# Transposing a convolution's output by DMA through HBM in place of TensorE, in a fused convolution and feed-forward kernel

## The chip, the cores and the metric

The kernel runs on one core of one Trainium2 chip. The metric is device time in microseconds (us), the median of several runs of the whole launch. A profile of one execution shows the engines apart: PE is TensorE's matmul stream and PEld its weight loads, DVE is VectorE, ACT is ScalarE, POOL is GpSimd, and SP is the engine that issues most of the DMAs. "SPq" rows are the DMA issues on SP.

## The reference

The input x is 8 sequences of 3904 rows of 192 features, in fp32. A softmax over 7 taps for each of 8 heads gives the weights of a causal convolution along the sequence: 24 features belong to one head and share its taps. What comes out goes, row by row, through a gated feed-forward network without a nonlinearity.

```python
# convolution: w = softmax(weight) of shape (8 heads, 7 taps), 6 rows of zeros ahead of each sequence
out = np.einsum('hk,bskhg->bshg', w, x_unf)      # then reshaped to (31232, 192)
# network
a = x @ w1            # 192 -> 1024
b = x @ w2            # 192 -> 1024
h = a * b @ w3        # 1024 -> 1024
return (h @ w_out)    # 1024 -> 192, fp32
```

## The kernel before

All matmuls are in bf16. The two last products are folded: the kernel multiplies w3 by w_out once (lines 305 to 324), so each row of a * b needs a single product with a 1024 x 192 matrix W.

**Two tilings.** The convolution works in 32 blocks of 976 rows (BLK = 8 windows of 122 rows). The network works in 61 chunks of 512 rows (CH). Between them lies a ring of 4096 columns, in which the convolved rows stand transposed: features on partitions, rows along the free axis.

**The convolution of a block** (`band_products`, lines 229 to 235, and `conv_pair`, lines 186 to 201). A window is 128 input rows on 128 partitions, 122 of them new. For each head a banded 128 x 122 matrix holds the taps. Eight matmuls (line 193), two heads to a PSUM bank, make all eight windows; four ACT copies (line 197) bring them to SBUF as bf16 into the tile `convo`, 122 partitions by 8 windows by 256 columns. Then one POOL copy (line 201) repeats features 128 to 191 in columns 192 to 255. After that the next block's x is cast to bf16 on POOL (line 180) and the load of x for the block three further on is issued on SP (line 76).

**The transposes of a block** (`transposes`, lines 237 to 239, and `transp`, lines 209 to 226). For each of two groups of 128 columns, eight TensorE transposes (line 213) write one PSUM bank, and DVE copies it to the ring (line 218). The first group gives xT0 (features 0 to 127), the second xT2 (features 128 to 191, twice). A third operand, xT1, is xT0 with its halves of 64 partitions exchanged: from block 2 on, two DMAs on SP make it out of xT0 (lines 223 and 224); for blocks 0 and 1, an ACT and a DVE copy do (lines 220 and 221).

**Why three operands.** In `first_product` (lines 261 to 276) a matmul for a takes partitions 0 to 63 and one for b takes partitions 64 to 127, side by side in TensorE's rows. Each of the three operands gives both a slice of 64 features. Eight groups of six matmuls (line 270) make one chunk; ACT copies a (line 275), and DVE multiplies it with b (line 276). `second_product` (lines 280 to 297) multiplies with W in two halves of 16 matmuls (line 289), ACT copies (line 292), and SP stores the chunk (line 294).

**The order is written out by hand.** Every engine executes its instructions in the order of the program. The main loop (lines 363 to 373) runs over chunks c = 3 to 60: `first_product(c)`, then a convolution step if one is due, the first half of `second_product(c - 3)`, a further step if due, the second half. The steps stand in a list (lines 241 to 247): the products of block it + 1 come ahead of the transposes of block it. A step is due in chunk c when chunk c + 2 needs it: what chunk c transposes is read for the first time by `first_product(c + 2)`. So in most pairs of chunks the first has both steps, the products of block it + 1 and the transposes of block it, and the second has none. Of the 32 transposes, those of blocks 0, 1 and 2 stand ahead of the loop, and those of blocks 3 to 31 in it.

**Waits between DMAs.** The program has eight DMA semaphores, used in turn; a DMA that reuses one waits on SP until the DMA that had it before has landed.

Of the kernel before, what the change touches and what calls it, by code (L numbers as in the profile page):

```python
# [10 lines left out]
BF16 = mybir.dt.bfloat16  # L11
# [6 lines left out]
def kernel(  # L18
# [10 lines left out]
    nc = tc.nc  # L29

    B, S, D = x.shape
# [6 lines left out]
    ST = 122  # L38
    NW = 8
    BLK = ST * NW  # L40
# [4 lines left out]
    RING = 8 * CH  # L45
    LAG = 3

    const = ctx.enter_context(tc.tile_pool(name="const", bufs=1))
    stage = ctx.enter_context(tc.tile_pool(name="stage", bufs=2))
    work = ctx.enter_context(tc.tile_pool(name="work", bufs=2))  # L50
    psum = ctx.enter_context(tc.tile_pool(name="psum", bufs=8, space=bass.MemoryType.PSUM))
    ctx.enter_context(tc.manual_schedule())

    def bank(shape, dtype, name):
        return psum.tile(shape, dtype, tag="bank", name=name)
# [51 lines left out]
    for jt in range(JT):  # L107
# [11 lines left out]
        out=dmask, in_=ones.unsqueeze(2).to_broadcast([128, K, ST]),  # L119
# [9 lines left out]
    for q, (c0, j0, n) in enumerate(QC):  # L129
# [6 lines left out]
        out=wsb, in0=wsb, in1=wmax.unsqueeze(2).to_broadcast([128, H, K]),  # L136
# [6 lines left out]
        out=wsb, in0=wsb, in1=wsum.unsqueeze(2).to_broadcast([128, H, K]),  # L143
# [21 lines left out]
                nc.scalar.copy(out=dst, in_=src)  # L165


    xT0 = const.tile([128, RING], BF16)
    xT1 = const.tile([128, RING], BF16)
    xT2 = const.tile([128, RING], BF16)  # L170
    xT = (xT0, xT1, xT2)

    def cast_x(it, first=False):
        xb = work.tile([128, NW, D], BF16, tag="xb", bufs=2, name="xb")
# [6 lines left out]
        return xb  # L181

    convo_of = {}
    xb_of = {}

    def conv_pair(it, t):
        if t == 0:
            convo_of[it] = work.tile([128, NW, D + 64], BF16, tag="convo", bufs=2, name="convo")
        convo, xb = convo_of[it], xb_of[it]
        cps = bank([128, 2, NW, G], FP32, "cps")  # L190
        for r in range(2):
            h = 2 * t + r
            nc.tensor.matmul(  # L193
                cps[0:ST, r], Aband[:, h, :], xb[:, :, h * G:(h + 1) * G],
                start=True, stop=True)
        dst = convo[0:ST, :, 2 * t * G:(2 * t + 2) * G]
        nc.scalar.copy(  # L197
            out=dst.rearrange("s b (r g) -> s r b g", r=2), in_=cps[0:ST])
        if t == 3:
            del xb_of[it]  # L200
            nc.gpsimd.tensor_copy(out=convo[0:ST, :, D:D + 64], in_=convo[0:ST, :, 128:192])  # L201

    def ring_spans(t0, n):
        a = t0 % RING
        if a + n <= RING:
            return [(0, a, n)]
        return [(0, a, RING - a), (RING - a, 0, n - (RING - a))]

    def transp(it, k):
        convo = convo_of[it]  # L210
        tps = bank([128, BLK], BF16, "tps")
        for w in range(NW):
            nc.tensor.transpose(  # L213
                out=tps[:, w * ST:(w + 1) * ST],
                in_=convo[0:ST, w, 128 * k:128 * (k + 1)],
                identity=ident[0:ST, 0:ST])
        for src, a, n in ring_spans(it * BLK, BLK):
            nc.vector.tensor_copy(out=xT[2 * k][:, a:a + n], in_=tps[:, src:src + n])  # L218
            if k == 0 and it < 2:
                nc.scalar.copy(out=xT1[0:64, a:a + n], in_=tps[64:128, src:src + n])  # L220
                nc.vector.tensor_copy(out=xT1[64:128, a:a + n], in_=tps[0:64, src:src + n])  # L221
            elif k == 0:
                nc.sync.dma_start(out=xT1[0:64, a:a + n], in_=xT0[64:128, a:a + n])
                nc.sync.dma_start(out=xT1[64:128, a:a + n], in_=xT0[0:64, a:a + n])
        if k == 1:
            del convo_of[it]


    def band_products(it):
        for t in range(4):  # L230
            conv_pair(it, t)
        if it + 1 < NB:
            xb_of[it + 1] = cast_x(it + 1)
        if it + 3 < NB:
            xr_of[it + 3] = load_x(it + 3)

    def transposes(it):
        transp(it, 0)
        transp(it, 1)

    steps = [(band_products, 0), (transposes, 0), (band_products, 1)]
    ready = {0: 2}
    for it in range(1, NB):
        if it + 1 < NB:
            steps.append((band_products, it + 1))
        steps.append((transposes, it))
        ready[it] = len(steps)
# [159 lines left out]
```

## Time and profile before

| what | value |
|---|---|
| median of 3 runs | 586.35 us (586.03 to 587.52) |
| span of the profiled execution, first to last instruction | 584.6 us |
| granted TensorE clock, mean | 0.996 |
| PE transposes, line 213 | 512 matmuls, mean 222 ns of one |
| DVE copies of them, line 218, 128 x 976 | 50, mean 661 ns of one |
| POOL copy, line 201 | 32, mean 612 ns of one |
| DMA | 64.17 MB, mean 110 GB/s |

The profile gives one time for the execution on the device and another for the span from the first instruction to the last; the runs' median lies 1.75 us above the span. A row of the timeline starts with start and duration in us, then the engine, the line and operation, output and input, and how many instructions are merged in the row. In square brackets stands how long the engine was idle before it and who released it. The duration of one matmul includes its way through the array; neighbours overlap, so what matmuls take of the time is read from their starts, or from the chain of work that ended last, where each has its own share alone. A row of DMA issues ends with the size in KB (of 1024 bytes) and the median us from issue to landing. A row of windows gives the busy time of PE, PEld, DVE, ACT and POOL in a stretch, then the granted TensorE clock, the share of 16 DMA engines, and GB/s.

### The profile page before, as it was taken

The numbers are of one execution on the slowest core, as the hardware profiler recorded it, in microseconds if no ns is written. First come the engines' busy times: TensorE is split into PE (matmuls) and PEld (weight loads), VectorE is DVE, ScalarE is ACT, GpSimd is POOL, SyncE is SP. The second block draws the span as 40 slices with busy tenths as digits, with TensorE's granted clock in tenths as the row PEclk, the third lists the DMA queues.
The fourth block names the chain that finished last, engine by engine and source line by source line (L and its number), as shares of the span: only waits on it lengthen the run. The fifth ranks groups of instructions, "written<-read, shape, count | busy, mean of one in ns | idle before, by whom it ended". The sixth has DMA issues, their size and how long they took to land.

```text
span 584.6 us, 14554 instructions
## 1 busy us (share of the span) xinstructions
PE 557.5 (95%) x5776; PEld 358.3 (61%) x5776; DVE 374.9 (64%) x590; ACT 405.3 (69%) x761; POOL 78.8 (13%) x94
## 2 busy tenths in 40 slices
PE   0869999999999999999999999999999999999997
PEld 0346765666656756656656656666666666566657
DVE  6447576575676666675765666766766756766760
ACT  2567686677676776776776776776866777766672
POOL 3352101111101201111001111021011111010000
PEclk9989999999999999999999999999999999999999
DMA  7992033244343442344342343353332441221213
GB/s 192 349 287 73 15 113 106 69 123 127 89 120 98 128 126 74 98 126 116 91 126 72 100 126 99 111 143 93 115 106 67 126 126 35 66 73 46 72 56 109
DMA packets 74793, 64.17 MB, mean 110 GB/s; under 512 B 3690, under 2 KB 72932, under 8 KB 74724
## 3 DMA queue, kind: packets, MB, share of 16 engines
q1 hardware_dynamic: 74100, 62.42, 36.9%
q10 hardware_dynamic: 624, 0.82, 0.6%
q8 instruction: 45, 0.74, 0.6%
q14 instruction: 24, 0.20, 0.1%
HBM read 31.74 MB, written 23.99 MB: 95 GB/s over the span
## 4 chain that ended last, share of the span: by engine, by line
PE 91%; issue 3%; DVE 2%; POOL 1%; ACT 1%; DMA 1%; ACTq 0%; SPq 0%; POOLq 0%; DVEq 0%
PE pa L270 52%; PE ops L289 28%; PE tps L213 4%; PE cps L193 4%; PE pb L270 1%; PE wps L322 1%; DMA xr<-in_x_dram 1%; DVE abT L276 1%; POOL xb L180 0%; PE w3ps L313 0%; POOL wb L332 0%; DVE cprod L152 0%; ACT w3b L307 0%; DVE xT L218 0%; DVE w3T L316 0%
## 5 line engine op out<-in xcount | busy, mean ns | idle before, releaser
L276 DVE TENSOR_TENSOR abT<-asb,pb 128x512 bf16<-128x512 bf16 x488 | 318.1, 687 | 141.3 <-PE pb L270 136.8
L270 PE MATMUL pa<-xT,wb 64*128 64x512 bf16 x1464 | 330.2, 378 | 1.2 <-ACT xT L220 0.7
L270 PE MATMUL pb<-xT,wb 64*128 64x512 bf16 x1464 | 330.2, 378 | 0.6 <-DVE xT L221 0.3
L275 ACT CAST asb<-pa 128x512 bf16<-128x512 f32 x488 | 285.2, 586 | 48.0 <-PE pb L270 21.9
L270 PEld LDWEIGHTS <-wb 64*128 64x128 bf16 x2928 | 139.2, 94 | 173.6 <-issue 17.6
L289 PE MATMUL ops<-W_sb,abT 128*128 128x192 bf16 x1952 | 175.5, 246 | 0.0
L289 PEld LDWEIGHTS <-abT 128*128 128x128 bf16 x1952 | 159.7, 98 | 12.3 <-issue 12.3
L292 ACT COPY osb<-ops 128x384 f32<-128x384 f32 x122 | 58.3, 478 | 104.3 <-PE ops L289 104.1
L201 POOL COPY convo<-convo 122x512 bf16<-122x512 bf16 x32 | 19.6, 612 | 433.6 <-ACT convo L197 417.6
L218 DVE COPY xT<-tps 128x976 bf16<-128x976 bf16 (+7 forms) x78 | 40.7, 569 | 44.3 <-PE tps L213 44.3
L197 ACT CAST convo<-cps 122x384 bf16<-122x384 f32 x128 | 52.3, 504 | 2.7 <-PE cps L193 2.7
L193 PE MATMUL cps<-xb,Aband 128*122 128x192 bf16 x256 | 29.3, 259 | 18.8 <-POOL xb L178 15.3
L180 POOL CAST xb<-xr 128x1536 bf16<-128x1536 f32 x31 | 45.5, 1467 | 0.0
L193 PEld LDWEIGHTS <-Aband 128*122 128x122 bf16 x256 | 22.9, 138 | 31.7 <-issue 17.0
L213 PE MATMUL tps<-ident,convo 122*128 122x122 bf16 x512 | 34.4, 222 | 1.4 <-ACT convo L197 1.3
L213 PEld LDWEIGHTS <-convo 122*128 122x128 bf16 x512 | 31.0, 101 | 2.4 <-ACT convo L197 1.6
L322 PE MATMUL wps<-wo_b,w3T 128*128 128x192 bf16 x64 | 6.6, 246 | 1.2 <-DVE w3T L316 1.1
L316 DVE COPY w3T<-w3ps 128x1024 bf16<-128x1024 bf16 x8 | 5.4, 689 | 2.9 <-PE w3ps L313 2.9
L324 ACT CAST W_sb<-wps 128x192 bf16<-128x192 f32 x8 | 2.5, 319 | 6.2 <-PE wps L322 6.2
L322 PEld LDWEIGHTS <-w3T 128*128 128x128 bf16 x64 | 5.1, 98 | 1.6 <-DVE w3T L316 1.6
L138 ACT ACT_TABLE_LOAD x1 | 1.3, 1283 | 6.3 <-DMA xr<-in_x_dram 6.3
L165 ACT COPY Aband<-cband 32x152 bf16<-32x152 bf16 (+1 forms) x4 | 1.2, 306 | 6.0 <-DVE cband L158 5.9
(36 smaller groups left out, 44.3 us busy)
## 6 DMA issues: line engine op xcount, KB each, us to landing
xr<-in_x_dram SPq DMA_DIRECT2D x31, 768.0 KB, 5.4
out_dram<-osb SPq DMA_DIRECT2D x61, 384.0 KB, 3.0
xT<-xT SPq DMA_DIRECT2D x46, 122.0 KB, 2.3
w3f<-in_moe_w_dram SPq DMA_DIRECT2D x8, 512.0 KB, 9.8
wo_f<-in_moe_w_out_dram SPq DMA_DIRECT2D x1, 768.0 KB, 9.1
xr<-in_x_dram SPq DMA_DIRECT2D x1, 672.0 KB, 7.6
w0f<-in_moe_w_dram ACTq DMA_DIRECT2D x2, 128.0 KB, 6.0
w1f<-in_moe_w_dram ACTq DMA_DIRECT2D x2, 128.0 KB, 5.9
```

Of the source, the lines that this page charges most:

```text
L180: nc.gpsimd.tensor_copy(out=xb, in_=xr)
L193: nc.tensor.matmul(cps[0:ST, r], Aband[:, h, :], xb[:, :, h * G:(h + 1) * G], start=True, stop=True)
L197: nc.scalar.copy(out=dst.rearrange("s b (r g) -> s r b g", r=2), in_=cps[0:ST])
L201: nc.gpsimd.tensor_copy(out=convo[0:ST, :, D:D + 64], in_=convo[0:ST, :, 128:192])
L213: nc.tensor.transpose(out=tps[:, w * ST:(w + 1) * ST], in_=convo[0:ST, w, 128 * k:128 * (k + 1)], identity=ident[0:ST, 0:ST])
L218: nc.vector.tensor_copy(out=xT[2 * k][:, a:a + n], in_=tps[:, src:src + n])
L270: nc.tensor.matmul(dst, wb[k][rows, ft * 128:(ft + 1) * 128], xT[k][rows, r0:r0 + CH], start=(k == 0), stop=(k == 2))
L275: nc.scalar.copy(out=asb, in_=pa)
L276: nc.vector.tensor_tensor(out=ab[:, ft, :], in0=asb, in1=pb, op=ALU.mult)
L289: nc.tensor.matmul(ops[:, r, :], ab[:, jt, g * 128:(g + 1) * 128], W_sb[:, jt, :], start=(jt == 0), stop=(jt == JT - 1))
L292: nc.scalar.copy(out=osb[:, 2 * half:2 * half + 2, :], in_=ops)
L322: nc.tensor.matmul(wps, w3T[:, gt, :], wo_b[:, gt, :], start=(gt == 0), stop=(gt == JT - 1))
```

## The change

Blocks 0 and 1 stay as they are, with the exchange of halves on ACT and DVE. From block 2 on, POOL makes two more copies into `convo`, which becomes 384 columns wide: the columns 256 to 383 then hold features 0 to 127 with their halves exchanged. Two DMAs on SP (112 partitions and 10) write the block's 976 rows of 384 columns to a buffer in HBM, of which there are three. Where the transposes of the block stood, one transposing DMA on SP (two, where the block wraps round the ring's end) reads 976 x 384 from HBM and writes 128 partitions x 3 x 976 into the ring. The ring's three operands become one tile. The TensorE transposes, their DVE copies and the two exchanging DMAs are gone for these blocks.

The built program has SP's queue in this order for a pair of chunks: rows of block it + 1 (two DMAs), x of block it + 4, the transposing DMA of block it, the stores of two chunks. The rows wait for the last of the three POOL copies of block it + 1. The first matmul of `first_product(c + 2)` waits for the transposing DMA that was issued in chunk c.

```diff
+    dram = ctx.enter_context(tc.tile_pool(name="dram", bufs=3, space=bass.MemoryType.DRAM))
...
-    xT0 = const.tile([128, RING], BF16)
-    xT1 = const.tile([128, RING], BF16)
-    xT2 = const.tile([128, RING], BF16)
-    xT = (xT0, xT1, xT2)
+    xTa = const.tile([128, 3, RING], BF16)
+    xT = [xTa[:, k, :] for k in (0, 2, 1)]
+    xT1 = xT[1]
+
+    PE_BLOCKS = 2
+    C = 2 * D
...
-            convo_of[it] = work.tile([128, NW, D + 64], BF16, tag="convo", bufs=2, name="convo")
+            convo_of[it] = work.tile([128, NW, C], BF16, tag="convo", bufs=2, name="convo")
...
             nc.gpsimd.tensor_copy(out=convo[0:ST, :, D:D + 64], in_=convo[0:ST, :, 128:192])
+            if it >= PE_BLOCKS:
+                nc.gpsimd.tensor_copy(out=convo[0:ST, :, 256:320], in_=convo[0:ST, :, 64:128])
+                nc.gpsimd.tensor_copy(out=convo[0:ST, :, 320:384], in_=convo[0:ST, :, 0:64])
+                rows = dram.tile([NW, ST, C], BF16, tag="rows", bufs=3, name="rows")
+                rows_of[it] = rows
+                for a, b in ((0, 112), (112, ST)):
+                    nc.sync.dma_start(out=rows[:, a:b, :].rearrange("w s c -> s w c"),
+                                      in_=convo[a:b])
+                del convo_of[it]
...
-            if k == 0 and it < 2:
+            if k == 0:
                 nc.scalar.copy(out=xT1[0:64, a:a + n], in_=tps[64:128, src:src + n])
                 nc.vector.tensor_copy(out=xT1[64:128, a:a + n], in_=tps[0:64, src:src + n])
-            elif k == 0:
-                nc.sync.dma_start(out=xT1[0:64, a:a + n], in_=xT0[64:128, a:a + n])
-                nc.sync.dma_start(out=xT1[64:128, a:a + n], in_=xT0[0:64, a:a + n])
...
     def transposes(it):
+        if it >= PE_BLOCKS:
+            rows = rows_of.pop(it).rearrange("w s c -> (w s) c")
+            for src, a, n in ring_spans(it * BLK, BLK):
+                nc.sync.dma_start_transpose(out=xTa[:, :, a:a + n], in_=rows[src:src + n, :])
+            return
         transp(it, 0)
         transp(it, 1)
```

More of the change, by code (lines that the diff above doesn't have):

```diff
@@ L183 @@
     convo_of = {}
+    rows_of = {}
     xb_of = {}
```

## The prediction

> **What bounds the kernel now.** I read the shares of the engines first, then the chain of work that ended last.
>
> ```profile
> PE 557.5 (95%) x5776; PEld 358.3 (61%) x5776; DVE 374.9 (64%) x590; ACT 405.3 (69%) x761; POOL 78.8 (13%) x94
> ...
> PE 91%; issue 3%; DVE 2%; POOL 1%; ACT 1%; DMA 1%; ACTq 0%; SPq 0%; POOLq 0%; DVEq 0%
> ```
>
> PE sets the end nearly alone; ACT and DVE have about a third of the span to spare. So a matmul that goes is worth its full length, provided that its data still come in time. Next comes PE's timeline for one pair of chunks in mid-run:
>
> ```profile
> 248.12 0.39 PE L270 MATMUL pa<-xT,wb 64*128 64x512 bf16 x1
> ...
> 253.41 0.87 PE L193 MATMUL cps<-xb,Aband 128*122 128x192 bf16 x8
> 254.11 1.48 PE L289 MATMUL ops<-W_sb,abT 128*128 128x192 bf16 x16
> 255.43 1.02 PE L213 MATMUL tps<-ident,convo 122*128 122x122 bf16 x16
> 256.29 1.49 PE L289 MATMUL ops<-W_sb,abT 128*128 128x192 bf16 x16
> 257.71 0.39 PE L270 MATMUL pa<-xT,wb 64*128 64x512 bf16 x1
> ...
> 265.74 0.39 PE L270 MATMUL pa<-xT,wb 64*128 64x512 bf16 x1
> ```
>
> There is no gap. Call the start of this pair's first chunk S = 248.12; the pair lasts 265.74 - 248.12 = 17.62 us, and what is transposed in it is first read at its end. The start of the row at 256.29 less that of the row at 255.43 prices the 16 transposes; the chain of work gives the same.
>
> ```profile
> 273.21 0.86 PE tps L213 x16
> ```
>
> **What is removed.** 30 blocks x 0.86 = 25.8 us of PE, all on the path. DVE loses 30 x 2 x 0.66 = 40 us, which was off the path and brings nothing. SP loses the exchanging DMAs, which nobody waited for in mid-run. A pair shrinks to 17.62 - 0.86 = 16.76 us.
>
> **What is added, and its deadline.** The new path is long: convolution matmuls, ACT copies, three POOL copies, rows to HBM, then on SP's queue x of a later block and only then the transposing DMA. That DMA does not need block it + 1 itself, but it stands behind that block's rows on SP, so it inherits their wait. Its deadline is S + 16.76. ACT, POOL and SP in the same pair show where it can start:
>
> ```profile
> 253.99 1.64 ACT L197 CAST convo<-cps 122x384 bf16<-122x384 f32 x4
> ```
>
> ```profile
> 255.76 0.61 POOL L201 COPY convo<-convo 122x512 bf16<-122x512 bf16 x1 [15.59 <-ACT convo L197]
> 256.32 1.47 POOL L180 CAST xb<-xr 128x1536 bf16<-128x1536 f32 x1
> ```
>
> ACT ends at 255.63, the first POOL copy starts at 255.76, and the next instruction follows 0.56 us later. Two more copies make the last one end at 255.76 + 2 x 0.56 + 0.61 = 257.49; with about 0.1 us for the wake-up (255.63 to 255.76 above) the rows are issued at 257.6, that is S + 9.5. So 7.3 us remain for everything that the DMA engines have to do.
>
> Now the DMA engines. Before the change the store and the load of x are issued together, and the load lands behind the store:
>
> ```profile
> 248.73 0.38 SPq L294 DMA_DIRECT2D out_dram<-osb  x1
> 249.20 0.46 SPq L76 DMA_DIRECT2D xr<-in_x_dram  x1
> ```
>
> ```profile
> q1 hardware_dynamic: 74100, 62.42, 36.9%
> ...
> xr<-in_x_dram SPq DMA_DIRECT2D x31, 768.0 KB, 5.4
> out_dram<-osb SPq DMA_DIRECT2D x61, 384.0 KB, 3.0
> ```
>
> From the store's issue, 384 KB land after 3.0 us, and 1152 KB after 249.20 + 5.4 - 248.73 = 5.9 us. The further 768 KB took 2.9 us, which is 271 GB/s, and the fixed part is 3.0 - 0.393/0.271 = 1.55 us. After the change three transfers are issued together: rows 732 KB, x 768 KB, transposing read 732 KB. Rows and x take (0.750 + 0.786)/0.271 = 5.7 us.
>
> The transposing DMA is not in the trace. Bound from below: the same bytes at the same rate, 0.750/0.271 = 2.8 us. Bound from above: it moves pieces of 128 columns (256 bytes), 976 x 3 = 2928 of them; a piece of queue q1 took 0.369 x 584.6 x 16 / 74100 = 46.6 ns, at a mean of 842 bytes; if a small piece costs as much as such a large one, 2928 x 46.6 / 16 = 8.5 us. The nearest row is the load of x, same direction and nearly the same bytes, so I stay nearer the lower end, but three times the pieces must cost something: I take **4.0 us**. The ten-partition DMA of rows has 80 pieces: 0.2 us if they spread over all 16 engines, 80 x 46.6 = 3.7 us if they fall on one; I take it as part of the bytes and keep the other end for the range.
>
> The Trainium skill (Advanced Engine Details and Errata, section X-Bar Transpose) has such transposes as fast as plain DMAs, 350 to 400 GB/s. An estimate from it is 2 us in place of 4.0, and a sum near 613. The skill also holds a rule against this change (VectorE: DVE Perf Modes, Rules for kernel authors): transpose on TensorE where PSUM will do for the result. Its table there (The three transpose paths) has 1309 ns by DMA against 390 ns on TensorE for one 128x128 tile; worked out for 23 tiles one after the other, an estimate of 30 us and a sum near 1400. The trace's own TensorE row is 0.86/16 = 54 ns each, so its table is for single tiles, and no run here shows the DMA side.
>
> **The stall.** The transposing DMA lands at S + 9.5 + 1.55 + 5.7 + 4.0 = S + 20.75, or 4.0 us after the deadline. Behind the waiting matmul stands all of PE: the whole pair moves, and the next pair's convolution with it, so the loss comes again in each pair and nothing catches up. Blocks 3 to 31 are transposed in the main loop; where two neighbouring chunks both have one (twice), the second hides behind the first: 27 stalls, 27 x 4.0 = 108 us.
>
> **The clock.** The trace has one idle stretch of such a length, ahead of the third convolution:
>
> ```profile
> 33.60 1.44 PE L193 MATMUL cps<-xb,Aband 128*122 128x192 bf16 x8 [3.48 <-POOL xb L180]
> ```
>
> ```profile
> 33.60:35.00 1.40, 1.40 (x10) 1.38 (x10) 0.00 (x0) 0.83 (x3) 0.00 (x0) 0.50 1.11 326
> 35.00:37.00 2.00, 2.00 (x19) 1.54 (x17) 0.67 (x1) 1.21 (x4) 0.00 (x0) 0.57 1.11 326
> ```
>
> After 3.48 us of idleness the granted clock was 0.50, and it was full again before 37: about 3.4 us at half clock, 1.7 us lost. A stall of 4.0 us is just above that gap, so each pair loses between 0 and 1.7 us; I take half, 27 x 0.85 = 23 us.
>
> **Costs put at nothing.** POOL's 60 further copies (37 us in all) lie in POOL's idle time (13% busy) but for the 1.1 us already in the path. Ahead of the main loop they delay POOL's casts of w3 by up to 2 x 1.1 us; I take 0, because POOL there waited for PE. The stores come behind the transposing DMA on SP and land later, but the two output tiles give them a pair of chunks.
>
> **The sum.** 584.6 - 25.8 + 108 + 23 = 689.8 us of span; with the 1.75 us by which the median lies above the span, **691 us**. With the lower bound and no clock loss the stall is 2.8 us and the time 636. With 5.8 us for the DMA and the full clock loss it is 763. This case, 635 to 765: chance 0.55.
>
> **Rivals.**
> 1. *A small piece costs like a large one.* The DMA takes 8.5 us, the stall is 8.5 us, and the clock drops each time: 27 x 10.2 = 275, time 836; with part of the ten-partition end, up to 880. For it speaks that no plain DMA here has such small pieces in number; against it, that time per piece grows with its size in a plain copy. Chance 0.19.
> 2. *All is hidden* (the other side: faster). The three transfers, 2.286 MB, land within 7.3 us of the first rows. The page's best slice moved 349 GB/s:
>
> ```profile
> GB/s 192 349 287 73 15 113 106 69 123 127 89 120 98 128 126 74 98 126 116 91 126 72 100 126 99 111 143 93 115 106 67 126 126 35 66 73 46 72 56 109
> ```
>
> At that rate they need 1.55 + 6.55 = 8.1 us, the stall is 0.8 us and the time 583; at 400 GB/s or more nothing stalls, and it is 584.6 - 25.8 + 1.75 = 561. It decides from a stall of 25.8/27 = 0.96 us: below that the change wins. Against it: that slice loads weights in long pieces, while 768-byte rows moved at 271. Chance 0.16.
> 3. *The transposing DMA is a bottleneck of its own*, in its descriptors or in the crossing of partitions: with 20 us, the stall is 20 us and the clock drops, 27 x 21.7 = 586, time 1147. Nothing in the trace bounds it. Chance 0.10.
>
> **How the numbers follow.** The likeliest case gives 691. The range leaves out rival 3 (0.10) and reaches from the fully hidden case with a little room, 557, to the end of rival 1, 880. What a measurement of this kernel can tell from no change is about 0.3%: faster is rival 2 nearly whole, 0.15; same 0.01; slower 0.84.
>
> **What would show it.** Right: in PE's timeline a gap of some 4 us ahead of every second first matmul of line 270 (line 285 after), released by the transposing DMA; that DMA's row of about 10 to 11 us from issue to landing, where it waits behind rows and x; granted clock below 1 in many slices; ACT and DVE idle in the same gaps. Wrong: no gap there, or the gap released by POOL or ACT; a landing below 6 us, which would show that the queue does not make it wait; or a gap of over 10 us, which is rival 3.

## The result, and the profile after

The changed kernel takes 690.37 us (median of 4 runs, 686.73 to 697.06) against 586.2 us: a ratio of 1.1754, 95% interval 1.1712 to 1.1796. Its profiled execution spans 690.3 us. The forecast was 691, in the likeliest of its cases. That the total agrees does not yet show that its terms are right; two of them were off and made up for each other, as the experiments show. A run that took over 1.5% longer than the fastest run of its kernel is left out of the ratios and intervals, here and below: one of the changed kernel's four (697.06), and two of the four of "x behind" (605.35 and 606.95).

First the page of the changed kernel: shares of the engines, the granted clock in 40 slices, the main DMA queue, and the group of matmuls that waits.

```profile
PE 572.0 (83%) x5296; PEld 343.2 (50%) x5296; DVE 339.2 (49%) x516; ACT 405.8 (59%) x761; POOL 112.7 (16%) x154
...
PEclk9999899989998899998899989999988999899999
...
q1 hardware_dynamic: 187232, 99.90, 61.0%
...
L285 PE MATMUL pa<-xTa,wb 64*128 64x512 bf16 x1464 | 368.7, 410 | 92.7 <-DMA xTa<-rows 91.0
```

PE has 480 matmuls fewer, yet it is busy for 572.0 us in place of 557.5: the mean matmul of the first product takes 410 ns in place of 378, because the clock is low in many slices. And PE is no longer busy all the time: 91.0 us of idleness stand ahead of this group, released by the transposing DMA. The list of waits gives the number and the longest:

```profile
PE pa L285 <- DMA xTa<-rows: 91.0, 25, 5.8
```

PE's timeline in mid-run, from one first product through the next two that wait:

```profile
298.58 0.39 PE L285 MATMUL pa<-xTa,wb 64*128 64x512 bf16 x1
...
303.87 2.81 PE L304 MATMUL ops<-W_sb,abT 128*128 128x192 bf16 x32
312.37 0.60 PE L285 MATMUL pa<-xTa,wb 64*128 64x512 bf16 x1 [5.69 <-DMA xTa<-rows]
...
319.80 0.87 PE L197 MATMUL cps<-xb,Aband 128*122 128x192 bf16 x8
320.51 2.80 PE L304 MATMUL ops<-W_sb,abT 128*128 128x192 bf16 x32
323.24 0.39 PE L285 MATMUL pa<-xTa,wb 64*128 64x512 bf16 x1
...
328.53 2.81 PE L304 MATMUL ops<-W_sb,abT 128*128 128x192 bf16 x32
334.78 0.60 PE L285 MATMUL pa<-xTa,wb 64*128 64x512 bf16 x1 [3.44 <-DMA xTa<-rows]
```

Every second first product waits. Two durations are to be seen: the undisturbed one, 323.24 to 328.53, is 5.29 us; the one after a gap, 312.37 to 319.80, is 7.43 us. SP and POOL in the same stretch:

```profile
299.24 0.88 SPq L212 DMA_DIRECT2D rows<-convo  x2
300.16 1.47 SPq L77 DMA_DIRECT2D xr<-in_x_dram  x1
301.73 7.09 SPq L251 DMA_TRANSPOSE xTa<-rows  x1
308.92 1.07 SPq L309 DMA_DIRECT2D out_dram<-osb  x2
```

```profile
298.60 0.62 POOL L208 COPY convo<-convo 122x512 bf16<-122x512 bf16 x1
```

The last POOL copy ends at 299.22, the rows are issued at 299.24, and everything else follows from there. New in this view: the transposing DMA holds SP for 7.09 us, where a plain one holds it for about half a microsecond. In the trace's DMA records its pieces of 256 bytes run from 305.3 to 310.3, so SP is still held while most of them flow; over the pairs in mid-run the medians are 11.0 us from the rows' issue to the last piece, 6.1 us of them before the first piece, and 4.9 us between the first and the last.

The clock around the gap (busy PE, PEld, DVE, ACT, POOL; granted clock; DMA share; GB/s):

```profile
307.00:309.00 2.00, 0.00 (x0) 0.00 (x0) 0.00 (x0) 0.20 (x1) 0.00 (x0) 1.00 1.26 123
309.00:311.00 2.00, 0.00 (x0) 0.00 (x0) 0.00 (x0) 0.00 (x0) 0.00 (x0) 0.73 1.23 319
...
313.00:315.00 2.00, 2.00 (x12) 0.71 (x10) 0.52 (x1) 0.59 (x1) 0.00 (x0) 0.50 0.03 8
315.00:317.00 2.00, 2.00 (x14) 0.77 (x12) 0.85 (x2) 1.16 (x2) 0.00 (x0) 0.56 0.00 0
317.00:319.00 2.00, 2.00 (x22) 0.87 (x18) 1.76 (x3) 1.57 (x4) 0.00 (x0) 1.00 0.00 0
```

It drops within the gap and stays at half for some 4 us after PE has resumed: PE pays twice for the same wait.

### The profile page after: what moved, and what is told of

Read it like the earlier page. It is cut to its first block, busy times and chain, and to the rows that moved or that the text cites. A ratio compares the mean times of both kernels' runs of the same rounds, so it can differ in the third digit from the quotient of the medians.

```text
span 690.3 us, 13590 instructions
## 1 busy us (share of the span) xinstructions
PE 572.0 (83%) x5296; PEld 343.2 (50%) x5296; DVE 339.2 (49%) x516; ACT 405.8 (59%) x761; POOL 112.7 (16%) x154
## 5 line engine op out<-in xcount | busy, mean ns | idle before, releaser
L285 PE MATMUL pa<-xTa,wb 64*128 64x512 bf16 x1464 | 368.7, 410 | 92.7 <-DMA xTa<-rows 91.0
L285 PE MATMUL pb<-xTa,wb 64*128 64x512 bf16 x1464 | 368.5, 410 | 0.6 <-DVE xTa L234 0.3
L285 PEld LDWEIGHTS <-wb 64*128 64x128 bf16 x2928 | 149.8, 101 | 294.9 <-DMA xTa<-rows 87.1
L304 PE MATMUL ops<-W_sb,abT 128*128 128x192 bf16 x1952 | 170.8, 246 | 0.0
L205 POOL COPY convo<-convo 122x512 bf16<-122x512 bf16 x32 | 19.7, 615 | 465.8 <-issue 437.1
L207 POOL COPY convo<-convo 122x512 bf16<-122x512 bf16 x30 | 18.5, 617 | 0.0
L208 POOL COPY convo<-convo 122x512 bf16<-122x512 bf16 x30 | 18.5, 617 | 0.0
L82 POOL MEMSET xr<- 6x192 f32 x7 | 1.7, 248 | 47.0 <-DMA xr<-in_x_dram 47.0
L231 DVE COPY xTa<-tps 128x976 bf16<-128x976 bf16 x4 | 2.7, 668 | 9.4 <-PE tps L226 9.3
L226 PE MATMUL tps<-ident,convo 122*128 122x122 bf16 x32 | 3.8, 306 | 1.4 <-ACT convo L201 1.3
```

Source lines behind the costliest of these rows:

```text
L207: nc.gpsimd.tensor_copy(out=convo[0:ST, :, 256:320], in_=convo[0:ST, :, 64:128])
L208: nc.gpsimd.tensor_copy(out=convo[0:ST, :, 320:384], in_=convo[0:ST, :, 0:64])
L285: nc.tensor.matmul(dst, wb[k][rows, ft * 128:(ft + 1) * 128], xT[k][rows, r0:r0 + CH], start=(k == 0), stop=(k == 2))
L304: nc.tensor.matmul(ops[:, r, :], ab[:, jt, g * 128:(g + 1) * 128], W_sb[:, jt, :], start=(jt == 0), stop=(jt == JT - 1))
```

## The experiments

The theory: nothing is too slow in itself. The transposing DMA is issued behind the next block's POOL copies, rows and x, lands after its deadline, and PE stalls in each pair of chunks; the stall also drops the clock. Rivals: the DMA engines or SP are the bound; the new traffic or the crossing writes slow other engines; the clock has no part in it. Medians of all runs, with the ratio to the kernel before:

| run | median us | ratio, 95% interval | PE waits for the transposing DMA |
|---|---|---|---|
| changed kernel | 690.37 | 1.1754 (1.1712 to 1.1796) | 91.0 us, 25 times |
| due a chunk earlier | 567.92 | 0.9689 (0.9671 to 0.9707) | 4.8 us, once |
| x behind | 603.03 | 1.0206 (1.0159 to 1.0254) | 28.8 us, 20 times |
| transposing DMA first | 561.01 | 0.9563 (0.9546 to 0.9581) | none |
| filler matmuls | 679.15 | 1.1593 (1.1526 to 1.166) | 29.9 us, 21 times |
| traffic alone | 586.53 | 1.0002 (0.9991 to 1.0014) | nobody reads it |
| copies on DVE | 668.0 | 1.1369 (1.132 to 1.1419) | 70.8 us, 24 times |

### Due a chunk earlier

```diff
-        need = steps_for(min(c + 2, NCH - 1))
+        need = steps_for(min(c + 3, NCH - 1))
```

> One number is changed: a convolution step is due when chunk c + 3 needs it, and not chunk c + 2. The same DMAs stand in the same order on SP; only the reader comes one chunk (about 8 us) later. Theory (a deadline missed by 3 to 6 us in each pair of chunks, and the clock drop that the gap brings): the waits of line 285 for the transposing DMA, 91 us in the changed kernel, go to nearly 0, the granted clock goes back to 0.99, and the time is 584.6 - 25.8 + 1.75 = 561 us, 558 to 570. Rival 1 (the DMA engines or SP are the bound: one pair's transfers take as long as a pair): a later reader changes the first pair alone, and the time stays at 670 to 690. Rival 2 (the transposing DMA slows TensorE or the copies while it writes): between 600 and 690, with matmuls longer than 378 ns at full clock.

567.92 us. Of its PE waits for this DMA, one is left:

```profile
PE pa L285 <- DMA xTa<-rows: 4.8, 1, 4.8
```

That one is the pair at the head of the main loop, whose step cannot be due earlier than the loop begins; it costs 4.8 us, and the clock that drops with it another 1.6 us in the first product behind it. That is nearly all of the 7 us by which the time lies above that of the next but one experiment. The DMAs are the same, in the same order, and take as long as before (11.2 us from the rows' issue to the last piece, median, beside 11.0). So the pace is not set by DMA engines or SP: a reader that comes 8 us later finds the data there. So rivals 1 and 2 of the expectation fall.

### x behind the transposing DMA

```diff
-        if it + 3 < NB:
+        if it + 3 < NB and it < 4:
             xr_of[it + 3] = load_x(it + 3)
...
                 nc.sync.dma_start_transpose(out=xTa[:, :, a:a + n], in_=rows[src:src + n, :])
+            if 3 <= it and it + 4 < NB:
+                xr_of[it + 4] = load_x(it + 4)
             return
```

> In the main loop the load of x is issued behind the transposing DMA, not ahead of it; deadline and all else as in the changed kernel. Theory (the transposing DMA lands late because rows and x stand ahead of it): about 2.9 us of each gap go (768 KB at 271 GB/s), gaps of 3.6 us on average become some 0.7 us, too short for the clock to drop, and the time is 561 + 27 x 0.7 = 580 us, 565 to 600. Rival 1 (the DMA engines or SP are the bound): the same bytes and issues in each pair, so 670 to 690. Rival 3 (SP needs 5 to 7 us to issue the transposing DMA whatever stands ahead, and its data end about 1.3 us after that): the issue starts 1.5 us earlier and nothing more is won, so 640 to 660.

603.03 us over all four runs; the two that the ratio of 1.0206 rests on took 596.24 and 600.72, at the upper end of the expected 565 to 600. Most of the loss is gone; what is left, by the interval of 1.0159 to 1.0254, lies on both sides of 2%. The trace is of the longest run (606.95), so its waits are rather too long than too short. From the rows' issue to the last piece it is 7.6 us in it in place of 11.0, so 3.4 us are won where 2.9 were expected. SP shows it too: with less ahead, the transposing DMA holds SP for 4.95 us.

```profile
339.59 0.88 SPq L212 DMA_DIRECT2D rows<-convo  x2
340.57 4.95 SPq L251 DMA_TRANSPOSE xTa<-rows  x1
```

What is left is 28.8 us of waits, 1.4 us on average where 0.7 was expected, and the clock still drops at seven of them. In about half of the pairs PE resumes 0.5 to 0.6 us after the last piece, in most of the others 2.0 to 2.2 us after it; the expectation had only a single value in mind.

The DMA records show what goes with the difference. Each transposing DMA ends with 16 landings on its semaphore, and PE resumes when the last of them has come. In the fast cases all 16 come within 0.6 us of the last piece. In most of the slow ones 15 do, and the sixteenth comes about 2.0 us after the last piece. Each time a packet of 16 or 8 KB of the queues that the page calls "instruction", a load of the program's own code by its name, was moving when the last piece came or had ended less than 0.15 us before. In the six traces in which the network reads what the transposing DMA writes, this holds for all 54 late cases (a last landing over 0.8 us after the last piece), and for only 10 of the 125 prompt ones. So late releases go with loads of code. No run moved these loads, so that they are the cause is likely but not shown.

Rival 3 of the expectation, which had SP's hold as a fixed length, falls.

### The transposing DMA first

```diff
-        if it + 1 < NB:
-            steps.append((band_products, it + 1))
-        steps.append((transposes, it))
+        if it > 2:
+            steps.append((transposes, it))
+        if it + 1 < NB:
+            steps.append((band_products, it + 1))
+        if it <= 2:
+            steps.append((transposes, it))
         ready[it] = len(steps)
```

> In the list of steps the transposes of block it stand ahead of the products of block it + 1, so the transposing DMA is issued at the start of its chunk, without the wait for the next block's POOL copies and ahead of that block's rows and x. The deadline is as in the changed kernel. Theory: it lands some 7 us after the chunk's start, 10 us ahead of its deadline; no gap, full clock, 561 us (558 to 570). Rival 1 (the DMA engines or SP are the bound): 670 to 690. A middle value would mean that SP, held for 5 to 7 us by the transposing DMA, now makes rows or stores late.

561.01 us, as the sum without stalls has it, and faster than the kernel before by 4.4% (ratio 0.9563, 0.9546 to 0.9581). The SP queue, which can be set beside the one above:

```profile
256.56 0.37 SPq L312 DMA_DIRECT2D out_dram<-osb  x1
257.10 4.01 SPq L251 DMA_TRANSPOSE xTa<-rows  x1
266.65 0.87 SPq L212 DMA_DIRECT2D rows<-convo  x2
267.57 1.54 SPq L77 DMA_DIRECT2D xr<-in_x_dram  x1
```

The DMA is issued at the head of its chunk (which began at 255.95), its rows were written a pair earlier, and its last piece comes at 262.6, 10 us before the pair ends at 272.68. PE's timeline is closed again:

```profile
255.95 0.39 PE L288 MATMUL pa<-xTa,wb 64*128 64x512 bf16 x1
...
261.24 1.49 PE L307 MATMUL ops<-W_sb,abT 128*128 128x192 bf16 x16
262.57 0.82 PE L197 MATMUL cps<-xb,Aband 128*122 128x192 bf16 x8
263.23 1.48 PE L307 MATMUL ops<-W_sb,abT 128*128 128x192 bf16 x16
264.64 0.39 PE L288 MATMUL pa<-xTa,wb 64*128 64x512 bf16 x1
...
269.93 2.81 PE L307 MATMUL ops<-W_sb,abT 128*128 128x192 bf16 x32
272.68 0.39 PE L288 MATMUL pa<-xTa,wb 64*128 64x512 bf16 x1
```

The pair lasts 272.68 - 255.95 = 16.73 us, as against the 16.76 worked out. This is the fastest kernel of the study, and the same instructions and bytes as in the changed kernel: only their order on the queues differs.

### Filler matmuls ahead of the wait

```diff
+    due, n = set(), done[0]
+    for c in range(LAG, NCH):
+        m = steps_for(min(c + 2, NCH - 1))
+        if m > n:
+            due.add(c + 2)
+            n = m
+
+    def filler(n):
+        fps = bank([128, CH], FP32, "fps")
+        for _ in range(n):
+            nc.tensor.matmul(fps, ident, wb[0][:, 0:CH], start=True, stop=True)
...
+        if c + 1 in due and c not in due:
+            filler(14)
```

The set `due` holds the chunks whose first product waits for a transposing DMA.

> The changed kernel with 14 further matmuls of 512 columns (about 3.0 us at full clock, results not used) ahead of each first product that waits for a transposing DMA. Theory (the gap is set by the DMA's landing, and some 40 us of the loss are the clock that drops after it): the added matmuls, some 27 x 3.0 = 81 us of PE work, fit into the gaps; the gaps that are left are mostly under 3 us, the clock stays near 1, and the time falls by 20 to 45 us, to 645 to 670. Rival 4 (the clock is no part of the loss): the time stays at 690. Rival 5 (PE is the bound and the gaps are a seeming of the trace): 690 + 81 = 771.

679.15 us. 378 added matmuls, 27 x 14 x 0.216 = 82 us of PE work, make the kernel 11 us faster, so PE is not the bound, and the clock is part of the loss. The expected 20 to 45 us were not reached. In the changed kernel 18 first products behind a gap took longer than the undisturbed 5.28 us, by 37.9 us in all; here four do, by 6.7 us, so 31 us of clock loss are saved. But ahead of the first products now stand 82 us of filler and 29.9 us of waits, 112 us in place of 91.0, so 21 us are given back. Some 12 of these arise at six pairs whose gap in the changed kernel was under 2 us, shorter than the filler; the rest was not traced. That leaves 10, near the 11 measured. A gap of less than 3 us still drops the clock sometimes (the shortest that did so in this trace was 2.13 us, at 411.72):

```profile
299.83 3.19 PE L388 MATMUL fps<-wb,ident 128*128 128x512 bf16 x14
305.62 0.39 PE L285 MATMUL pa<-xTa,wb 64*128 64x512 bf16 x1 [2.60 <-DMA xTa<-rows]
...
312.59 0.87 PE L197 MATMUL cps<-xb,Aband 128*122 128x192 bf16 x8
```

```profile
305.00:307.00 2.00, 1.38 (x10) 0.59 (x12) 0.00 (x0) 0.31 (x1) 0.00 (x0) 0.77 1.10 373
307.00:309.00 2.00, 2.00 (x12) 0.63 (x10) 1.09 (x2) 0.87 (x2) 0.00 (x0) 0.50 0.06 20
```

### The traffic alone

The kernel before, with the new work added at the end of the transposes, and its result in a buffer that is not read.

```diff
+            if it >= 2:
+                nc.gpsimd.tensor_copy(out=convo[0:ST, :, 256:320], in_=convo[0:ST, :, 64:128])
+                nc.gpsimd.tensor_copy(out=convo[0:ST, :, 320:384], in_=convo[0:ST, :, 0:64])
...
         transp(it, 1)
+        convo = convo_of.pop(it)
+        if it >= 2:
+            rows = dram.tile([NW, ST, 2 * D], BF16, tag="rows", bufs=3, name="rows")
+            rows_of[it] = rows
+            for a, b in ((0, 112), (112, ST)):
+                nc.sync.dma_start(out=rows[:, a:b, :].rearrange("w s c -> s w c"),
+                                  in_=convo[a:b])
+        if it >= 3:
+            rows = rows_of.pop(it - 1).rearrange("w s c -> (w s) c")
+            nc.sync.dma_start_transpose(out=xSa, in_=rows)
```

> The kernel before, with its TensorE transposes, DVE copies and exchanging DMAs, and on top of it the new work with nobody waiting for it: the two POOL copies, the rows to HBM, and from block 3 on the transposing DMA of the block before, into a buffer that is not read. Theory (the new work is slow only because first products wait for it): 586 us, 584 to 590. Rival 2 (the traffic or the writes of the transposing DMA slow the engines): 600 or more. Between: SP, held for some 4 to 7 us by each transposing DMA, makes the exchange of halves or x late, and the gaps are released by those DMAs.

586.53 us, a ratio of 1.0002 (0.9991 to 1.0014). Its page shows 170 to 220 GB/s in most slices, where the kernel before moved 70 to 130, and PE does not notice:

```profile
PE 557.8 (95%) x5776; PEld 358.3 (61%) x5776; DVE 374.9 (64%) x590; ACT 405.3 (69%) x761; POOL 112.4 (19%) x154
...
GB/s 187 344 297 124 11 219 189 188 170 197 177 225 187 171 284 190 177 181 190 196 200 204 174 184 171 213 222 221 216 208 166 179 190 128 167 174 147 133 100 109
```

Matmuls, DVE and ACT are as long as before. So neither the traffic nor the crossing writes nor the POOL copies cost anything where nobody waits for them.

### The copies on DVE

```diff
-            nc.gpsimd.tensor_copy(out=convo[0:ST, :, D:D + 64], in_=convo[0:ST, :, 128:192])
+            nc.vector.tensor_copy(out=convo[0:ST, :, D:D + 64], in_=convo[0:ST, :, 128:192])
```

and the two further copies in the same way.

> The changed kernel with the three copies into convo on DVE in place of POOL; the rows wait for DVE then. DVE idles there, and a copy of it should take about half of POOL's 0.62 us or less. Theory (POOL's copies lie on the path, cps to rows is 4.1 us of it): the rows are issued 0.8 to 1.2 us earlier, each of some 27 gaps shrinks by as much, and some fall below what drops the clock: 690 - 27 x 1.0 - 5 to 15 = 648 to 668 us. Rival 1 (the DMA engines or SP set the pace): 685 to 692.

668.0 us, at the upper edge of the expectation. A copy takes 0.28 to 0.35 us on DVE in place of 0.62, and from the convolution's first matmul to the rows' issue it is 3.08 us in place of 4.10:

```profile
PE pa L285 <- DMA xTa<-rows: 70.8, 24, 6.0
```

The waits are 20.2 us shorter, and the time is 22.4 us shorter, where 25 waits times the 1.02 us won ahead of the DMA would make 25: most of what is taken off the chain comes off the end. The clock loss changed little (34.9 us in first products in place of 37.9); its expected 5 to 15 us were not to be had while gaps of about 3 us remain.

## Why the prediction was right, step by step

- **What is removed, 25.8 us of PE.** Right: without stalls the kernel is 586.1 - 561.0 = 25.1 us faster.
- **The rows are issued at S + 9.5.** Right: 5.28 us of first product and 4.10 us to the rows make 9.4 at full clock. That the transposing DMA inherits this wait through SP's order is shown by the experiment that issues it first.
- **From the rows' issue to PE, 1.55 + 5.7 + 4.0 = 11.25 us.** Right as a sum: 11.0 us to the last piece and, mostly, 0.5 us more until PE resumes. The parts are not what was drawn: 6.1 us in place of 7.25 until the first piece, and then pieces for 4.9 us in place of 4.0. For the last block, which has nothing ahead, they take 3.0 us, 250 GB/s, close to the lower bound of 2.8 us. So the prediction's rival 1 fails: a piece of 256 bytes does not cost like a large one (18 ns in the records, the median, where one of 768 bytes takes 36). From its own issue the DMA takes 8.5 us to its last piece and not the 10 to 11 that the prediction named as a sign, because SP reaches it only 2.5 us after the rows' issue. That SP is held for 5 to 8 us was not foreseen; here nothing urgent stood behind it.
- **The stall, 27 x 4.0 = 108 us.** The mechanism is right, the size was 91.0 us in 25 waits, 3.6 us each. In mid-run the mean is 4.4 us, a little over the forecast, where one DMA transposes the block, and 2.4 us for the six blocks that wrap round the ring's end: the reader is released there after the first of two DMAs, which the prediction left out of its sum. The last blocks, which have no x load ahead, had a gap of under 1 us or none.
- **The clock, 27 x 0.85 = 23 us.** Too small. With 584.6 - 25.8 + 91.0 = 649.8 us, 690.3 - 649.8 = 40.5 us are left, and most of it is seen directly: after 18 of the 25 waits the first product took 6.8 to 8.2 us in place of 5.28, 37.9 us in all. "Between 0 and 1.7 us" was wrong as a bound, since it came from one event of 3.4 us: in the changed kernel's trace half of the stretches at half clock last 6.8 us, and up to 2.9 us were lost after one gap. This error and that of the stall, 17 us each, cancel in the total; that it came out within 1 us of the forecast is luck.
- **Costs put at nothing.** Right: traffic, POOL copies and stores behind a transposing DMA cost nothing in the experiment with the traffic alone.
- **Rival 2, all hidden,** did not come about in this order of the queue; with the deadline moved, or the order turned, it is exactly what happens, and its 561 us was the right price. **Rival 3** is refuted: alone, the transposing DMA is about as fast as a plain load, 250 GB/s beside 271.

On the rules of the Trainium skill: that such transposes are as fast as plain DMAs (Advanced Engine Details and Errata, X-Bar Transpose) agrees in kind with the 250 GB/s of the last block, which is below its 350 to 400, and not with 732 KB in 4.9 us in mid-run, 153 GB/s. The prediction's estimate of 30 us for 23 tiles one after the other did not come about. The rule to transpose on TensorE where PSUM will do (VectorE: DVE Perf Modes, Rules for kernel authors) held for the changed kernel and fails for the one with the DMA first: there TensorE is the bound, and 0.86 us a block on it are worth more than a DMA that is hidden.

Two things stay open: whether the loads of code are what delays PE's release in some pairs by 1.5 us, as the records suggest, and what stretches the transposing DMA's own 3.0 us to 4.9 behind other transfers.

## What to carry to other kernels

Work moved from the busiest engine to DMAs won here only where the transfer was issued a full latency ahead of its reader: write down the chain from the first input to the landing, with every wait that stands ahead on the issuing queue, and compare it with the distance to the reader. An order of steps that suited an engine's own work (next block's products ahead of this block's transposes) can be the wrong one for a DMA that does not need those products; turning two steps moved this kernel from 690 to 561 us. A stall that comes again in each iteration can also cost the clock that drops in it, here 38 to 40 us beside 91.

## What the runs showed of the hardware that was not expected

- A transposing DMA of 976 x 384 bf16 holds SP for 3.4 us for the last block, whose rows are long written, and with medians of 4.1 us behind a store, 4.9 us behind rows, and 6.1 us behind rows and x; a plain DMA holds it for about 0.5 us (median).
- Stretches at half clock last 3.4 or 6.8 us in the trace. A PE gap of 2.13 us was enough for one (filler matmuls), while gaps of 3.30 and 3.48 us in the changed kernel passed without one, so the length of the gap alone does not decide.
- A transposing DMA's last landing came mostly 0.5 us after its last piece; in 54 of the 64 cases in which a load of code was moving there, it came 0.9 to 2.2 us after it.
- DVE copies 122x512 bf16 from SBUF to SBUF in 0.28 us where POOL takes 0.62 us.
